# Ordering two products into one PSUM bank: a VectorE copy as a fence, or a drain in TensorE's own queue

## The chip, the cores and the metric

The kernel runs on one core of a Trainium2 chip. The metric is the device time of one execution in microseconds (us); the time of a kernel is the median of several executions. Beside the times stands a profile of one execution: every instruction of every engine with its start and length. The engines are TensorE (PE in the profile, PEld for its weight loads, which share its queue), VectorE (DVE), ScalarE (ACT), GpSimd (POOL), and SyncE (SP), which issues the DMAs. Each has its own queue, in which instructions start in order; engines wait for each other through semaphores.

## What is computed

A retention layer over 8 batches, 8 heads, 576 positions and head width 64, and then a feed-forward block over its 4608 rows:

```python
scores = scale * np.matmul(q, k.transpose(0, 1, 3, 2))
ret = scores * Dmat[None, :, :, :]        # Dmat: gamma ** (i - j) below the diagonal, else 0
attn = np.matmul(ret, v)                  # -> x, one row of 512 for each batch and position
h = x @ w_in                              # 512 -> 1024
e = np.exp(h - h_max); sm = e / (np.sum(e, axis=-1, keepdims=True) + 1e-09)
solu = h * sm
ln = (solu - mu) / np.sqrt(var + 1e-06) * g_ln
out = ln @ w_out                          # 1024 -> 512
```

Inputs and output are float32; the kernel multiplies in float16 and sums in float32.

## The kernel before

The 576 positions of a batch are cut into chunks of 128 and a last one of 64. A pair n holds one chunk of each of two batches, four groups of five, so 20 pairs; every fifth is the short one. A pair gives two row tiles of 128 rows (a short pair gives one), 36 tiles m in all.

Inside a chunk retention is worked out directly, and what came before it enters through a running state (64 by 64 for each head) that decays from chunk to chunk. So x of a pair is the sum of two products, in the same PSUM bank:

- the state products, step `xs` (line 374): the decayed state s16 of the chunk before, times the turned q. They need neither scores nor masks of this pair. The first chunk of a batch has no state, so its x has no such product.
- the value products, step `xv` (line 432): the masked scores `ret` times v. They are 32 matmuls of a 64 by 64 weight block for a full pair, 16 for a short one or for one batch of pair 0.

PE's array is worked in quarters here (64*64 in the profile). For a head the two products take their weights from different rows and both write the same bank. The kernel keeps them apart: the last state product has written before the first value product starts. Before the change the step `fx` (line 393) sees to that: a VectorE copy of a few columns of the bank, which waits for the state products because it reads what they write, and which the value products wait for because they write what it reads. What it copies, the tile `fence`, is read by nobody.

Around it, for each pair: load q, k, v (lines 187 and 180); cast and scale them to float16 (`cast`, lines 216 and 219, mostly on GpSimd); turn q and k (line 242 on PE and `back` at lines 134 and 136 out of PSUM, or a DMA at line 265); score products (line 311); two masks on VectorE, `m0` and `m1` (line 346, tile ret); new states (line 408 on PE, `t` at line 454 on VectorE, `decay` at line 458). Then for each tile: copy x out of PSUM and turn it into weights (`xT`, lines 134 and 136), w_in products (line 517), row maximum (line 540, tile nm), exp (line 565), h times e (line 595, tile u), moments (lines 602, 609, 617, 624, 632), transposes (line 643) and their copy (uT), w_out products (line 669), scaling (lines 685 and 689), store (line 700). `warm` (line 775) multiplies zeros.

The order is written out by hand: PLAN is one list of words, `name:pair.half/banks` with an engine behind @, and `follow` calls the step of each word in turn. Every engine's queue holds its instructions in the order of that list; semaphores are put in where an instruction reads or overwrites what another engine made. 20 words are `fx`: one for the second half of pair 0 and one for each later pair. Some stand right behind their `xs`, others several words later, and between `fx` and `xv` there is mostly other work for PE. On VectorE most stand behind the pair's masks; those of pairs 4 and 13 stand ahead of another pair's mask, and that of pair 0 ahead of its own.

Of the kernel before, what the change touches and what calls it, by code (L numbers as in the profile page):

```python
# [33 lines left out]
def kernel(  # L34
# [357 lines left out]
    @step  # L392
    def fx(n, j, eng, bs):

        bs = [T["x", n, x] for x in meets(n, j)]
        nc.vector.tensor_copy(
            out=buf("fence", 0, 1, [P, 2, 4], FP)[:, 0 : len(bs)], in_=banks(bs)[:, :, 0:512:128]
        )

    @step  # L400
    def kp(n, j, eng, bs):
        k16, v16 = t16("k", n), t16("v", n)

        def one(x, s, hp):
            r = slice(64 * x, 64 * x + 64)
            o = pb[:, bs[x if j is None else 0], 0:256].rearrange("p (a d) -> p a d", a=4)
            for e in range(2):
                nc.tensor.matmul(
                    out=o[64 * e : 64 * e + 64, hp], lhsT=k16[r, s, 2 * hp + e],
                    rhs=v16[r, s, 2 * hp + e], start=s == 0 and hp == 0, stop=True,  # L410
                    skip_group_check=True,
                )
# [360 lines left out]
    def warm(k, j, eng, bs):  # L773
# [9 lines left out]
        xv:0.0/4 tq:0.1/6 qT:0.1@v t:0.0@s s16:0.0@v warm:4/7 xs:0.1/5 fx:0.1 xT:0@s sc:0.1/0123  # L783
        m0:0.1 gl cw:0.1@s mm1:0.0/67 cw:1.1@s mm1:0.1 m1:0.1 warm:7/4 xv:0.1 cw:2.0@v wo:0 cw:3.0@s
        xT:1@v kp:0.1/4 cw:2.1@s mm1:0.2 s32:0.0@g cw:3.1@s mm1:0.3 max:0 mm1:1/01 t:0.1 max:1 q:1@g
        k:1@g warm:7/3 tk:1/2 exp:0 solu:0 nmu:0 w1:0.0 exp:1 solu:1 nmu:1 uc:1 wo:1 kT:1@s tq:1/3
        qT:1@s warm:4/6 sc:1/4523 m1:1 wo:2 m0:1 v:1@g warm:1/0 kp:1/67 t:1.0@s lp:1/0 s16:1.0@g
        s32:1.0@g xs:1/1 fx:1 xv:1/2 g32 uc:0 ws:2@v sq:1 wo:3 ws:7@v ws:6@g lv:2 ws:1@s lk:2 ws:3@s
        uT:1@v w1:0.1 t:1.1 s16:0.1@g s32:0.1@g s32:1.1@g lp:0/3 w2:0.1 xT:2@s mm1:2/45 ws:4@v
        ws:0@s lq:2 ws:5@s mm2:1/2 v:2@g max:2 exp:2 solu:2 nmu:2 lk:3 mean/0 k:2@s pow:0.1 uc:2  # L790
        uT:0@v osb:1@s kp:2/67 t:2.0 evm@s ce:1 ce:2 warm:3/4 lp:2/0 q:2@g s32:2.0@g tk:2/4 sq:0
        w2:0.0 s16:2.0@g lv:3 kT:2@s tq:2/5 qT:2@s warm:3/2 sc:2/2345 t:2.1 m0:2 xT:3@s xs:2/67
        uT:2@s s16:1.1@g m1:2 k:3@s fx:2 mm1:3/01 max:3 v:3@g kp:3/23 t:3.0 xv:2 xT:4@s xT:5@v ce:4
        exp:3 solu:3 nmu:3 s32:3.0@g tk:3/4 t:3.1 pow:0.0 mm2:0/5 osb:0@s lq:4 uc:3 kT:3@s mm1:4/67
        lq:3 q:3@g tq:3/5 max:4 qT:3@s lp:3/0 uT:3@s mm2:2/1 sc:3/2345 ce:0 mm2:3/0 ce:6 exp:4
        solu:4 sq:3 m1:3 m0:3 sq:2 mm1:5/67 lk:5 k:5@s lv:5 q:4@g tq:4/2 s16:3.0@g lk:4 qT:4@s lq:7
        xs:3/45 v:5@g w1:1 w2:1 lq:5 k:4@g tk:4/3 pow:1 osb:2@s max:5 exp:5 fx:3 lv:6 warm:1/2 xv:3
        st:0 kp:5/12 kT:4@v xT:7@s v:6@g t:5.0@s nmu:4 uc:4 lp:4/3 sq:4 lk:6 xT:6@v mm1:6/45 lk:7
        solu:5 s32:5.0@g osb:3@s nmu:5 uT:4@s uc:5 max:6 sq:5 lv:4 mm1:7/67 lp:5/0 t:5.1 lq:6 lq:10
        q:5@g w1:2 exp:6 tq:5/1 max:7 st:1 uT:5@s s16:2.1@g tk:5/3 k:6@g lv:7 exp:7 mm2:4/2 qT:5@s  # L800
        solu:6 lp:6/0 uT:6@s sc:4/45 ce:3 w2:2 pow:2 osb:4@s solu:7 kT:5@s s16:5.0@g m0:4 nmu:6
        mm2:5/1 osb:5@s ce:5 nmu:7 s16:3.1@g xs:4/67 fx:4 sc:5/4523 m0:5 m1:5 v:4@g xv:4 xT:8@s
        xs:5/0 fx:5 ce:7 st:4 sq:6 lp:7/1 w1:3 uT:7@s st:2 lq:9 mm1:8/67 max:8 kp:6/23 st:3 sq:7
        xv:5/1 xT:9@s lq:8 q:6@g t:6.0@s s32:6.0@v t:6.1 s16:6.1@v lv:9 lk:9 exp:8 st:5 wx xT:10@s
        solu:8 nmu:8 w1:4 mm2:7/4 s16:6.0@g w2:3 pow:3 s32:5.1@g tk:6/5 kT:6@v mm1:9/23 max:9 sq:8
        w2:4 v:7@g pow:4 mm1:10/01 k:9@g tq:6/5 max:10 exp:9 solu:9 lv:8 qT:6@s mm2:6/6 s16:5.1@g
        osb:7@s q:7@g exp:10 osb:6@v st:6 lp:8/7 lk:8 nmu:9 lq:11 sc:6/4523 uT:8@s m0:6 sq:9 k:7@g
        xs:6/6 mm2:8/7 m1:6 lk:10 fx:6 xv:6/2 lv:10 solu:10 nmu:10 q:9@v kp:7/45 t:7.0 q:8@g lp:9/3
        s32:7.0@g xT:11@s tk:7/0 kT:7@s mm1:11/12 s16:7.0@v uT:9@v v:8@g lk:11 osb:8@s xT:12@s
        max:11 sq:10 w1:5 exp:11 w2:5 pow:5 t:7.1 lp:10/0 uT:10@v solu:11 mm1:12/67 lk:12 tq:7/3  # L810
        qT:7@s mm2:9/4 sc:7/0123 max:12 m0:7 k:8@g tk:8/5 osb:9@s mm2:10/4 lv:11 exp:12 w1:6 m1:7
        kT:8@s lp:11/5 solu:12 st:8 q:10@g osb:10@s xs:7/01 fx:7 uT:11@v tq:9/2 qT:9@s nmu:11 st:7
        tq:8/3 xv:7 xT:13@s kp:8/67 s32:6.1@v s16:7.1@v v:10@g lp:12/2 mm1:13/45 t:8.0 qT:8@s
        xT:14@v s16:8.0@g nmu:12 s32:8.0@v t:8.1 s16:8.1@v max:13 sq:12 st:9 lv:12 sc:8/0167 m1:8
        sq:11 w2:6 v:9@g m0:8 uT:12@s exp:13 solu:13 pow:6 mm2:11/3 osb:11@v mm2:12/2 xs:8/01 fx:8
        mm1:14/67 xv:8 max:14 osb:12@s lp:13/4 uT:13@v dq:10 xT:15@s tk:9/5 exp:14 kT:9@s mm1:15/23
        xT:16@v k:10@g lq:12 nmu:13 sq:13 solu:14 nmu:14 sc:9/45 m0:9 mm1:16/01 xs:9/67 lq:13 dk:10
        v:11@g lq:15 max:15 lk:13 sq:14 fx:9 exp:15 st:11 max:16 solu:15 nmu:15 st:10 q:11@g lp:14/4
        st:12 xv:9 xT:17@s k:11@g mm2:13/5 exp:16 dk:11 q:12@g kp:10/67 t:10.0@s uT:14@s dq:11 sq:15
        lq:14 w1:7 w2:7 pow:7 lv:14 solu:16 osb:13@s mm1:17/23 lp:15/4 s32:10.0@g t:10.1 uT:15@s  # L820
        sc:10/0167 max:17 exp:17 lp:16/5 uT:16@s mm2:14/4 m0:10 m1:10 lv:13 s16:10.0@g k:12@s lk:14
        lv:15 xs:10/5 dk:12 fx:10 kp:11/01 t:11.0@s s16:10.1@g solu:17 nmu:16 xv:10/6 xT:18@s k:13@g
        q:13@g s32:11.0@g t:11.1 xT:19@v mm1:18/67 lp:17/5 uT:17@s nmu:17 osb:14@v s32:11.1@g dq:12
        s32:10.1@g max:18 sc:11/2301 exp:18 m1:11 s16:11.0@g xs:11/4 m0:11 w1:9 st:13 mm2:15/5 dq:13
        mm1:19/01 solu:18 lp:18/2 fx:11 xv:11/3 sq:17 k:14@g w2:9 v:12@v max:19 s16:11.1@g sq:16
        xT:21@s mm2:16/6 xT:20@v w1:8 w2:8 st:14 pow:9 exp:19 solu:19 nmu:19 uT:18@s pow:8 q:14@g
        osb:16@s osb:15@s mm1:20/34 max:20 sc:12/6701 m1:12 m0:12 exp:20 mm2:17/2 v:13@g nmu:18
        st:16 mm2:18/5 dk:13 solu:20 w1:10 osb:17@v sq:18 st:15 kp:12/01 t:12.0 s32:12.0@v mm1:21/67
        t:12.1 max:21 v:14@g lv:16 s16:12.0@g lk:15 sq:19 w2:10 pow:10 k:15@g lp:19/4 uT:19@s
        tk:14/3 kT:14@v tq:14/2 qT:14@v s16:12.1@v nmu:20 xs:12/01 lq:16 exp:21 q:16@g fx:12 lk:16  # L830
        solu:21 nmu:21 w1:11 mm2:19/4 xv:12 du:21 kp:13/23 k:16@g t:13.0 s32:13.0@v t:13.1 osb:18@s
        lp:20/5 xT:22@s mm1:22/67 sq:21 xT:23@s sc:13/2301 max:22 m1:13 m0:13 uT:20@s q:15@g
        osb:19@s lq:17 exp:22 sq:20 st:18 mm1:23/45 max:23 exp:23 mm2:21/0 w2:11 pow:11 mm2:20/1
        solu:22 nmu:22 s16:13.0@g sq:22 solu:23 dk:15 nmu:23 xs:13/23 fx:13 sc:14/67 lv:17 m0:14
        s16:13.1@g xs:14/45 fx:14 xv:13 xT:24@s xv:14 xT:25@v v:15@g kp:15/67 xT:26@v st:17 osb:21@s
        v:17@v w1:12 t:15.0@s s16:15.0@g s32:15.0@v mm1:25/23 v:16@g t:15.1 s32:15.1@g osb:20@s
        max:25 sq:23 w2:12 st:19 pow:12 du:23 mm1:24/45 exp:25 max:24 exp:24 mm2:23/0 osb:23@s
        s16:15.1@v du:22 mm2:22/1 dq:15 solu:25 sc:15/6723 solu:24 nmu:24 dq:16 m1:15 m0:15 q:17@g
        xs:15/0 fx:15 mm1:26/45 max:26 kp:16/23 du:24 xv:15/6 xT:27@v osb:22@s t:16.0@s s32:16.0@g
        exp:26 lp:25/1 t:16.1 uT:25@s solu:26 xT:28@s nmu:25 lk:18 sq:24 k:18@g nmu:26 dk:16  # L840
        mm1:27/67 max:27 mm1:28/23 max:28 exp:27 lp:26/1 solu:27 uT:26@s sc:16/4501 m0:16 s16:16.0@g
        xs:16/6 sq:25 m1:16 fx:16 w1:14 mm2:24/7 lq:19 sq:26 exp:28 solu:28 nmu:28 xv:16/0 lk:17
# [83 lines left out]
```

## Time and profile before

| | us |
|---|---|
| median of 3 runs | 230.87 |
| lowest and highest run | 229.31, 231.76 |
| the profiled execution, its own time | 231.2 |
| its span, first to last instruction | 229.5 |
| VectorE's copies of x into xT (line 136, 12 of them), busy | 8.5 |
| masks (line 346, 38 of them), busy | 42.7 |
| value products (line 432, 576 matmuls), busy | 12.6 |
| state products (line 374, 256 matmuls), busy | 9.0 |

"Busy" is the time in which at least one instruction of the group ran. Matmuls overlap in the array and their ends are modelled, so 576 value products of 216 ns each are busy for 12.6 us only. The chain of waits is followed back from the last instruction: at each step to what released it, or to the instruction before it in its queue; its shares say which engine ended last and for how long. In a view that names gaps, "[0.51 <-PE pb L374]" is the time that the engine stood idle before the instruction and what ended it. A "q" behind an engine's name marks its sequencer, which issues the instructions and itself runs some, drains among them.

### The profile page before, as it was taken

The numbers are of one execution on the slowest core, as the hardware profiler recorded it, in microseconds if no ns is written. First come the engines' busy times: TensorE is split into PE (matmuls) and PEld (weight loads), VectorE is DVE, ScalarE is ACT, GpSimd is POOL, SyncE is SP. The second block draws the span as 40 slices with busy tenths as digits, with TensorE's granted clock in tenths as the row PEclk, the third lists the DMA queues.
The fourth block names the chain that finished last, engine by engine and source line by source line (L and its number), as shares of the span: only waits on it lengthen the run. The fifth ranks groups of instructions, "written<-read, shape, count | busy, mean of one in ns | idle before, by whom it ended". The sixth has DMA issues, their size and how long they took to land.

```text
span 229.5 us, 7260 instructions
## 1 busy us (share of the span) xinstructions
PE 210.5 (92%) x2994; PEld 115.1 (50%) x2994; DVE 198.0 (86%) x346; ACT 152.9 (67%) x267; POOL 133.2 (58%) x181
## 2 busy tenths in 40 slices
PE   7999798999999999998998999998978689999992
PEld 2454543654565456564555544644434345555461
DVE  4568967999998899899999889999998988797971
ACT  2354647568898786657689566786547867857861
POOL 2585658887677498484687366487834083630230
PEclk9999979999999999999999999999999999999998
DMA  6999999999676999999898999999949997907044
GB/s 124 261 322 253 320 286 246 268 231 312 147 227 194 256 215 312 286 274 246 120 325 140 223 224 204 299 188 299 128 82 159 239 203 225 237 3 141 0 184 137
DMA packets 93265, 49.00 MB, mean 214 GB/s; under 512 B 37680, under 2 KB 87088, under 8 KB 93104
## 3 DMA queue, kind: packets, MB, share of 16 engines
q1 hardware_dynamic: 93088, 48.51, 94.0%
q8 instruction: 23, 0.38, 0.7%
q14 instruction: 10, 0.08, 0.1%
q10 hardware_dynamic: 144, 0.03, 0.1%
HBM read 32.54 MB, written 9.44 MB: 183 GB/s over the span
## 4 chain that ended last, share of the span: by engine, by line
PE 43%; DVE 31%; issue 7%; POOL 6%; DMA 6%; SPq 3%; ACT 3%; DVEq 0%; ACTq 0%; POOLq 0%
PE pb L517 15%; PE pb L669 12%; DVE ret L346 8%; DVE u L595 6%; DVE nm L540 5%; PE pb L775 5%; DMA ring<-in_k_dram 3%; PE pb L432 3%; DMA ring<-in_v_dram 3%; PE pb L643 2%; POOL v L219 2%; DVE w_mid L767 2%; PE pb L242 2%; PE pb L374 2%; POOL s L458 1%
## 5 line engine op out<-in xcount | busy, mean ns | idle before, releaser
L517 PE MATMUL pb<-w_in,xT 128*128 128x512 f16 x232 | 56.0, 388 | 3.0 <-ACT xT L134 1.3
L669 PE MATMUL pb<-w_mid,uT 128*128 128x512 f16 (+1 forms) x248 | 55.5, 373 | 0.0
L565 ACT ACTIVATE e<-pb,nm 128x1024 f32<-128x1024 f32 (+1 forms) x37 | 40.5, 1095 | 20.6 <-DVE nm L540 19.9
L540 DVE TENSOR_REDUCE nm<-pb 128x1 f32<-128x1024 f32 x35 | 42.6, 1219 | 7.0 <-PE pb L517 6.6
L595 DVE SCALAR_TENSOR_TENSOR u<-pb,e 128x1024 f16<-128x1024 f32 (+1 forms) x37 | 43.8, 1187 | 2.6 <-ACT e L565 2.3
L219 POOL TENSOR_TENSOR v<-ring,small 128x512 f16<-128x512 f32 (+1 forms) x34 | 37.3, 1114 | 10.7 <-DMA ring<-in_v_dram 6.2
L346 DVE TENSOR_TENSOR ret<-pb,keep 128x1024 f16<-128x1024 f32 (+2 forms) x38 | 42.7, 1158 | 0.8 <-PE pb L311 0.5
L517 PEld LDWEIGHTS <-xT 128*128 128x128 f16 x280 | 25.9, 99 | 34.1 <-ACT xT L134 2.6
L669 PEld LDWEIGHTS <-uT 128*128 128x128 f16 x296 | 27.6, 98 | 29.3 <-issue 0.6
L617 ACT ACTIVATE sq<-u,nmu 128x1024 f16<-128x1024 f16 (+1 forms) x31 | 34.9, 1125 | 4.3 <-DVE nmu L602 2.8
L219 POOL TENSOR_TENSOR q<-ring,small 128x512 f16<-128x512 f32 (+1 forms) x34 | 35.5, 1063 | 3.8 <-DMA ring<-in_q_dram 3.8
L458 POOL TENSOR_TENSOR s<-ts,small 128x256 f16<-128x256 f32 (+1 forms) x41 | 26.5, 659 | 15.5 <-DVE ts L454 8.1
L134 ACT CAST xT<-pb 128x512 f16<-128x512 f32 x24 | 17.1, 723 | 16.3 <-PE pb L432 16.2
L632 POOL TENSOR_TENSOR rs<-w,mhalf 128x2 f32<-128x2 f32 (+1 forms) x22 | 14.6, 664 | 19.2 <-DVE w L624 17.6
L689 ACT ACTIVATE osb<-pb,rs 128x512 f32<-128x512 f32 x26 | 17.7, 691 | 7.5 <-POOL rs L632 3.8
L136 POOL CAST k<-ring 128x1024 f16<-128x1024 f32 (+1 forms) x14 | 13.3, 948 | 14.6 <-DMA ring<-in_k_dram 13.8
L775 PE MATMUL pb<-zeros 128*128 128x512 f16 x58 | 17.2, 433 | 1.2 <-DVE zeros L874 1.2
L311 PE MATMUL pb<-qT,kT 64*64 64x128 f16 (+1 forms) x576 | 13.4, 217 | 3.5 <-DMA kT<-k 1.3
L591 POOL TENSOR_TENSOR w<-s 128x2 f32<-128x2 f32 (+1 forms) x22 | 4.8, 220 | 18.2 <-ACT e L565 18.2
L134 ACT COPY uT<-pb 128x512 f32<-128x512 f32 (+1 forms) x22 | 12.7, 577 | 3.7 <-PE pb L643 3.5
L311 PEld LDWEIGHTS <-kT 64*64 64x64 f16 x576 | 10.0, 106 | 9.7 <-issue 5.3
L643 PE MATMUL pb<-ident,u 128*128 128x128 f16 x184 | 13.8, 220 | 0.0
...
## 6 DMA issues: line engine op xcount, KB each, us to landing
...
```

What stands on the lines that cost most here:

```text
L134: nc.scalar.copy(out=out, in_=in_)
L219: vec(eng).tensor_tensor(out=t[:, s], in0=src[:, s], in1=by, op=ALU.mult)
L311: nc.tensor.matmul(out=scores(n, bs, e, hp, s)[c], lhsT=kt[r, s, hp, c], rhs=qt[r, 0:ns, hp, c], start=True, stop=True,)
L346: nc.vector.tensor_tensor(out=out, in0=src, in1=by, op=ALU.mult)
L458: vec(eng).tensor_tensor(out=s, in0=state("ts", n, x, FP), in1=gs.unsqueeze(2).to_broadcast([P, 4, D]), op=ALU.mult,)
L517: nc.tensor.matmul(out=pb[:, bs[i]], lhsT=s[:, d], rhs=w[:, d, i * 512 : (i + 1) * 512], start=r == 1, stop=r == 4,)
L540: nc.vector.tensor_reduce(out=tiny("nm", m, j), in_=h_of(m, j), axis=AX.X if j is not None else AX.XY, op=ALU.max, negate=True,)
L565: nc.scalar.activation(out=like_h(e_of(m), j), in_=h_of(m, j), func=ACT.Exp, bias=tiny("nm", m), accum_out=tiny("s", m, j),)
L595: nc.vector.scalar_tensor_tensor(out=like_h(u_of(m), j), in0=h_of(m, j), scalar=1.0, in1=like_h(e_of(m), j), op0=ALU.mult, op1=ALU.mult, a ...
L617: nc.scalar.activation(out=buf("sq", 0, 1, [P, DFF], F16)[:, cols(j)], in_=uc_of(m)[:, cols(j)], func=ACT.Square, accum_out=tiny("ss", m, ...
L669: nc.tensor.matmul(out=pb[:, bs[0], 0:w], lhsT=ut(m)[:, c], rhs=(w_out16 if m < RAW else w_mid16)[:, c, a : a + w], start=c == 0, stop=c = ...
L775: nc.tensor.matmul(out=pb[:, bs[0]], lhsT=zeros[:, 0:P], rhs=zeros, start=True, stop=True)
```

## The change

The step `fx` and its 20 words in PLAN go. In `xv` a drain of TensorE is put ahead of the matmuls wherever x already holds a state product; only the first half of pair 0 has none. PLAN is otherwise the same, word for word, so PE's matmuls and weight loads and the instructions of ScalarE, GpSimd and SyncE keep their order, and VectorE's queue loses 20 copies. The value products still wait for the masks and for v; a wait that was for the copy becomes one for the mask ahead of it. The second half of the value products of pair 2 then waits for the second mask by itself. Ten of the 20 drains stand behind matmuls on the whole array (128*128), ten behind matmuls on quarters (64*64).

```diff
     @step
-    def fx(n, j, eng, bs):
-
-        bs = [T["x", n, x] for x in meets(n, j)]
-        nc.vector.tensor_copy(
-            out=buf("fence", 0, 1, [P, 2, 4], FP)[:, 0 : len(bs)], in_=banks(bs)[:, :, 0:512:128]
-        )
-
-    @step
     def kp(n, j, eng, bs):
...
     @step
     def xv(n, j, eng, bs):
         new = [x for x in both(j) if ("x", n, x) not in T]
+        if len(new) < len(both(j)):
+
+            nc.tensor.drain()
         for x, b in zip(new, bs):
             T["x", n, x] = b
...
-        xs:1/1 fx:1 xv:1/2 g32 uc:0 ws:2@v sq:1
+        xs:1/1 xv:1/2 g32 uc:0 ws:2@v sq:1
```

More of the change, by code (lines that the diff above doesn't have):

```diff
@@ L782 @@
         warm:2/4 sc:0.0/2301 m0:0.0 v:0.1@g lv:1 warm:4/5 tk:0.1/4 kT:0.1@s kp:0.0/5 m1:0.0 warm:3/6
[L783 to L842, printed above, removed]
@@ L843 @@
-        xT:29@s q:19@v k:17@g xT:30@s kp:17/45 t:17.0 s32:17.0@v sq:28 lk:19 w1:13 w2:14 w2:13
-        pow:13 st:20 osb:24@s mm1:29/01 max:29 s32:16.1@g t:17.1 lv:18 mm1:30/23 max:30 exp:29
-        lp:28/6 solu:29 exp:30 st:21 dq:17 uT:28@s mm2:25/7 nmu:27 osb:25@s dk:17 sc:17/4501 k:19@s
-        m0:17 st:24 tk:18/6 pow:14 mm2:26/7 m1:17 s16:17.0@g xs:17/01 fx:17 sq:27 st:22 v:18@g
-        kp:18/45 kT:18@s xv:17 xT:31@s xT:32@s nmu:29 sq:29 w1:16 w1:15 s16:17.1@g du:27 solu:30
-        nmu:30 osb:26@v w2:15 s16:16.1@g pow:15 mm2:28/6 osb:28@s t:18.0 st:25 mm1:31/23 s32:18.0@v
@@ L849 @@
-        t:18.1 s16:18.1@g sq:30 max:31 exp:31 mm1:32/01 max:32 lq:18 w2:16 tk:19/7 kT:19@s tq:19/4
-        qT:19@s q:18@g s16:18.0@g tq:18/5 pow:16 solu:31 exp:32 du:29 solu:32 mm2:27/6 lp:30/7
-        qT:18@s uT:30@s sc:18/2345 m1:18 m0:18 xs:18/01 fx:18 st:23 osb:27@v mm2:29/7 lv:19 v:19@g
-        sc:19/23 m0:19 xv:18 xs:19/45 fx:19 st:26 st:27 lp:32/6 xv:19 w1:17 xT:33@s xT:34@v uT:32@s
-        nmu:31 sq:31 nmu:32 xT:35@v sq:32 mm1:33/23 max:33 mm1:34/01 max:34 exp:33 solu:33 exp:34
-        st:28 mm1:35.0/6 mm1:35.1/4 mm2:30/5 w1:18.1 w2:17 pow:17 nmu:33 max:35.0 max:35.1 nmm:35
@@ L855 @@
-        du:31 solu:34 nmu:34 mm2:31/2 osb:31@v mm2:32/3 lp:34/2 st:31 osb:29@s st:29 sq:33 exp:35.1
-        exp:35.0 solu:35.1 lp:35.1/7 solu:35.0 sadd:35 suadd:35 sq:34 osb:30@s w2:18.1 uT:34@s
-        w1:18.0 nmu:35 w2:18.0 lp:35.0/6 uT:35.0@v st:30 pow:18.0 osb:32@v lp:33/0 sq:35.1 mm2:34/1
-        pow:18.1 sq:35.0 uT:35.1@s mm2:35.0/4 uT:33@v mm2:33/5 st:32 ssadd:35 w1:19 w2:19 pow:19
-        osb:35.0@v osb:34@v st:35.0 st:34 mm2:35.1/4 osb:33@s osb:35.1@v st:33 st:35.1
+        xv:0.0/4 tq:0.1/6 qT:0.1@v t:0.0@s s16:0.0@v warm:4/7 xs:0.1/5 xT:0@s sc:0.1/0123 m0:0.1 gl
@@ new lines @@
+        cw:0.1@s mm1:0.0/67 cw:1.1@s mm1:0.1 m1:0.1 warm:7/4 xv:0.1 cw:2.0@v wo:0 cw:3.0@s xT:1@v
+        kp:0.1/4 cw:2.1@s mm1:0.2 s32:0.0@g cw:3.1@s mm1:0.3 max:0 mm1:1/01 t:0.1 max:1 q:1@g k:1@g
+        warm:7/3 tk:1/2 exp:0 solu:0 nmu:0 w1:0.0 exp:1 solu:1 nmu:1 uc:1 wo:1 kT:1@s tq:1/3 qT:1@s
+        warm:4/6 sc:1/4523 m1:1 wo:2 m0:1 v:1@g warm:1/0 kp:1/67 t:1.0@s lp:1/0 s16:1.0@g s32:1.0@g
+        xs:1/1 xv:1/2 g32 uc:0 ws:2@v sq:1 wo:3 ws:7@v ws:6@g lv:2 ws:1@s lk:2 ws:3@s uT:1@v w1:0.1
@@ new lines @@
+        t:1.1 s16:0.1@g s32:0.1@g s32:1.1@g lp:0/3 w2:0.1 xT:2@s mm1:2/45 ws:4@v ws:0@s lq:2 ws:5@s
+        mm2:1/2 v:2@g max:2 exp:2 solu:2 nmu:2 lk:3 mean/0 k:2@s pow:0.1 uc:2 uT:0@v osb:1@s kp:2/67
+        t:2.0 evm@s ce:1 ce:2 warm:3/4 lp:2/0 q:2@g s32:2.0@g tk:2/4 sq:0 w2:0.0 s16:2.0@g lv:3
+        kT:2@s tq:2/5 qT:2@s warm:3/2 sc:2/2345 t:2.1 m0:2 xT:3@s xs:2/67 uT:2@s s16:1.1@g m1:2
+        k:3@s mm1:3/01 max:3 v:3@g kp:3/23 t:3.0 xv:2 xT:4@s xT:5@v ce:4 exp:3 solu:3 nmu:3
+        s32:3.0@g tk:3/4 t:3.1 pow:0.0 mm2:0/5 osb:0@s lq:4 uc:3 kT:3@s mm1:4/67 lq:3 q:3@g tq:3/5
@@ new lines @@
+        max:4 qT:3@s lp:3/0 uT:3@s mm2:2/1 sc:3/2345 ce:0 mm2:3/0 ce:6 exp:4 solu:4 sq:3 m1:3 m0:3
+        sq:2 mm1:5/67 lk:5 k:5@s lv:5 q:4@g tq:4/2 s16:3.0@g lk:4 qT:4@s lq:7 xs:3/45 v:5@g w1:1
+        w2:1 lq:5 k:4@g tk:4/3 pow:1 osb:2@s max:5 exp:5 lv:6 warm:1/2 xv:3 st:0 kp:5/12 kT:4@v
+        xT:7@s v:6@g t:5.0@s nmu:4 uc:4 lp:4/3 sq:4 lk:6 xT:6@v mm1:6/45 lk:7 solu:5 s32:5.0@g
+        osb:3@s nmu:5 uT:4@s uc:5 max:6 sq:5 lv:4 mm1:7/67 lp:5/0 t:5.1 lq:6 lq:10 q:5@g w1:2 exp:6
+        tq:5/1 max:7 st:1 uT:5@s s16:2.1@g tk:5/3 k:6@g lv:7 exp:7 mm2:4/2 qT:5@s solu:6 lp:6/0
@@ new lines @@
+        uT:6@s sc:4/45 ce:3 w2:2 pow:2 osb:4@s solu:7 kT:5@s s16:5.0@g m0:4 nmu:6 mm2:5/1 osb:5@s
+        ce:5 nmu:7 s16:3.1@g xs:4/67 sc:5/4523 m0:5 m1:5 v:4@g xv:4 xT:8@s xs:5/0 ce:7 st:4 sq:6
+        lp:7/1 w1:3 uT:7@s st:2 lq:9 mm1:8/67 max:8 kp:6/23 st:3 sq:7 xv:5/1 xT:9@s lq:8 q:6@g
+        t:6.0@s s32:6.0@v t:6.1 s16:6.1@v lv:9 lk:9 exp:8 st:5 wx xT:10@s solu:8 nmu:8 w1:4 mm2:7/4
+        s16:6.0@g w2:3 pow:3 s32:5.1@g tk:6/5 kT:6@v mm1:9/23 max:9 sq:8 w2:4 v:7@g pow:4 mm1:10/01
+        k:9@g tq:6/5 max:10 exp:9 solu:9 lv:8 qT:6@s mm2:6/6 s16:5.1@g osb:7@s q:7@g exp:10 osb:6@v
@@ new lines @@
+        st:6 lp:8/7 lk:8 nmu:9 lq:11 sc:6/4523 uT:8@s m0:6 sq:9 k:7@g xs:6/6 mm2:8/7 m1:6 lk:10
+        xv:6/2 lv:10 solu:10 nmu:10 q:9@v kp:7/45 t:7.0 q:8@g lp:9/3 s32:7.0@g xT:11@s tk:7/0 kT:7@s
+        mm1:11/12 s16:7.0@v uT:9@v v:8@g lk:11 osb:8@s xT:12@s max:11 sq:10 w1:5 exp:11 w2:5 pow:5
+        t:7.1 lp:10/0 uT:10@v solu:11 mm1:12/67 lk:12 tq:7/3 qT:7@s mm2:9/4 sc:7/0123 max:12 m0:7
+        k:8@g tk:8/5 osb:9@s mm2:10/4 lv:11 exp:12 w1:6 m1:7 kT:8@s lp:11/5 solu:12 st:8 q:10@g
+        osb:10@s xs:7/01 uT:11@v tq:9/2 qT:9@s nmu:11 st:7 tq:8/3 xv:7 xT:13@s kp:8/67 s32:6.1@v
@@ new lines @@
+        s16:7.1@v v:10@g lp:12/2 mm1:13/45 t:8.0 qT:8@s xT:14@v s16:8.0@g nmu:12 s32:8.0@v t:8.1
+        s16:8.1@v max:13 sq:12 st:9 lv:12 sc:8/0167 m1:8 sq:11 w2:6 v:9@g m0:8 uT:12@s exp:13
+        solu:13 pow:6 mm2:11/3 osb:11@v mm2:12/2 xs:8/01 mm1:14/67 xv:8 max:14 osb:12@s lp:13/4
+        uT:13@v dq:10 xT:15@s tk:9/5 exp:14 kT:9@s mm1:15/23 xT:16@v k:10@g lq:12 nmu:13 sq:13
+        solu:14 nmu:14 sc:9/45 m0:9 mm1:16/01 xs:9/67 lq:13 dk:10 v:11@g lq:15 max:15 lk:13 sq:14
+        exp:15 st:11 max:16 solu:15 nmu:15 st:10 q:11@g lp:14/4 st:12 xv:9 xT:17@s k:11@g mm2:13/5
@@ new lines @@
+        exp:16 dk:11 q:12@g kp:10/67 t:10.0@s uT:14@s dq:11 sq:15 lq:14 w1:7 w2:7 pow:7 lv:14
+        solu:16 osb:13@s mm1:17/23 lp:15/4 s32:10.0@g t:10.1 uT:15@s sc:10/0167 max:17 exp:17
+        lp:16/5 uT:16@s mm2:14/4 m0:10 m1:10 lv:13 s16:10.0@g k:12@s lk:14 lv:15 xs:10/5 dk:12
+        kp:11/01 t:11.0@s s16:10.1@g solu:17 nmu:16 xv:10/6 xT:18@s k:13@g q:13@g s32:11.0@g t:11.1
+        xT:19@v mm1:18/67 lp:17/5 uT:17@s nmu:17 osb:14@v s32:11.1@g dq:12 s32:10.1@g max:18
+        sc:11/2301 exp:18 m1:11 s16:11.0@g xs:11/4 m0:11 w1:9 st:13 mm2:15/5 dq:13 mm1:19/01 solu:18
@@ new lines @@
+        lp:18/2 xv:11/3 sq:17 k:14@g w2:9 v:12@v max:19 s16:11.1@g sq:16 xT:21@s mm2:16/6 xT:20@v
+        w1:8 w2:8 st:14 pow:9 exp:19 solu:19 nmu:19 uT:18@s pow:8 q:14@g osb:16@s osb:15@s mm1:20/34
+        max:20 sc:12/6701 m1:12 m0:12 exp:20 mm2:17/2 v:13@g nmu:18 st:16 mm2:18/5 dk:13 solu:20
+        w1:10 osb:17@v sq:18 st:15 kp:12/01 t:12.0 s32:12.0@v mm1:21/67 t:12.1 max:21 v:14@g lv:16
+        s16:12.0@g lk:15 sq:19 w2:10 pow:10 k:15@g lp:19/4 uT:19@s tk:14/3 kT:14@v tq:14/2 qT:14@v
+        s16:12.1@v nmu:20 xs:12/01 lq:16 exp:21 q:16@g lk:16 solu:21 nmu:21 w1:11 mm2:19/4 xv:12
@@ new lines @@
+        du:21 kp:13/23 k:16@g t:13.0 s32:13.0@v t:13.1 osb:18@s lp:20/5 xT:22@s mm1:22/67 sq:21
+        xT:23@s sc:13/2301 max:22 m1:13 m0:13 uT:20@s q:15@g osb:19@s lq:17 exp:22 sq:20 st:18
+        mm1:23/45 max:23 exp:23 mm2:21/0 w2:11 pow:11 mm2:20/1 solu:22 nmu:22 s16:13.0@g sq:22
+        solu:23 dk:15 nmu:23 xs:13/23 sc:14/67 lv:17 m0:14 s16:13.1@g xs:14/45 xv:13 xT:24@s xv:14
+        xT:25@v v:15@g kp:15/67 xT:26@v st:17 osb:21@s v:17@v w1:12 t:15.0@s s16:15.0@g s32:15.0@v
+        mm1:25/23 v:16@g t:15.1 s32:15.1@g osb:20@s max:25 sq:23 w2:12 st:19 pow:12 du:23 mm1:24/45
@@ new lines @@
+        exp:25 max:24 exp:24 mm2:23/0 osb:23@s s16:15.1@v du:22 mm2:22/1 dq:15 solu:25 sc:15/6723
+        solu:24 nmu:24 dq:16 m1:15 m0:15 q:17@g xs:15/0 mm1:26/45 max:26 kp:16/23 du:24 xv:15/6
+        xT:27@v osb:22@s t:16.0@s s32:16.0@g exp:26 lp:25/1 t:16.1 uT:25@s solu:26 xT:28@s nmu:25
+        lk:18 sq:24 k:18@g nmu:26 dk:16 mm1:27/67 max:27 mm1:28/23 max:28 exp:27 lp:26/1 solu:27
+        uT:26@s sc:16/4501 m0:16 s16:16.0@g xs:16/6 sq:25 m1:16 w1:14 mm2:24/7 lq:19 sq:26 exp:28
+        solu:28 nmu:28 xv:16/0 lk:17 xT:29@s q:19@v k:17@g xT:30@s kp:17/45 t:17.0 s32:17.0@v sq:28
@@ new lines @@
+        lk:19 w1:13 w2:14 w2:13 pow:13 st:20 osb:24@s mm1:29/01 max:29 s32:16.1@g t:17.1 lv:18
+        mm1:30/23 max:30 exp:29 lp:28/6 solu:29 exp:30 st:21 dq:17 uT:28@s mm2:25/7 nmu:27 osb:25@s
+        dk:17 sc:17/4501 k:19@s m0:17 st:24 tk:18/6 pow:14 mm2:26/7 m1:17 s16:17.0@g xs:17/01 sq:27
+        st:22 v:18@g kp:18/45 kT:18@s xv:17 xT:31@s xT:32@s nmu:29 sq:29 w1:16 w1:15 s16:17.1@g
+        du:27 solu:30 nmu:30 osb:26@v w2:15 s16:16.1@g pow:15 mm2:28/6 osb:28@s t:18.0 st:25
+        mm1:31/23 s32:18.0@v t:18.1 s16:18.1@g sq:30 max:31 exp:31 mm1:32/01 max:32 lq:18 w2:16
@@ new lines @@
+        tk:19/7 kT:19@s tq:19/4 qT:19@s q:18@g s16:18.0@g tq:18/5 pow:16 solu:31 exp:32 du:29
+        solu:32 mm2:27/6 lp:30/7 qT:18@s uT:30@s sc:18/2345 m1:18 m0:18 xs:18/01 st:23 osb:27@v
+        mm2:29/7 lv:19 v:19@g sc:19/23 m0:19 xv:18 xs:19/45 st:26 st:27 lp:32/6 xv:19 w1:17 xT:33@s
+        xT:34@v uT:32@s nmu:31 sq:31 nmu:32 xT:35@v sq:32 mm1:33/23 max:33 mm1:34/01 max:34 exp:33
+        solu:33 exp:34 st:28 mm1:35.0/6 mm1:35.1/4 mm2:30/5 w1:18.1 w2:17 pow:17 nmu:33 max:35.0
+        max:35.1 nmm:35 du:31 solu:34 nmu:34 mm2:31/2 osb:31@v mm2:32/3 lp:34/2 st:31 osb:29@s st:29
@@ L860 @@
+        sq:33 exp:35.1 exp:35.0 solu:35.1 lp:35.1/7 solu:35.0 sadd:35 suadd:35 sq:34 osb:30@s
+        w2:18.1 uT:34@s w1:18.0 nmu:35 w2:18.0 lp:35.0/6 uT:35.0@v st:30 pow:18.0 osb:32@v lp:33/0
+        sq:35.1 mm2:34/1 pow:18.1 sq:35.0 uT:35.1@s mm2:35.0/4 uT:33@v mm2:33/5 st:32 ssadd:35 w1:19
+        w2:19 pow:19 osb:35.0@v osb:34@v st:35.0 st:34 mm2:35.1/4 osb:33@s osb:35.1@v st:33 st:35.1
     """
```

## The prediction, made before the changed kernel was run

> **What bounds the kernel now.** I read the page's busy times first, then its chain of waits by engine and line, then the two stretches in which VectorE (DVE) is fullest.
>
> ```profile
> span 229.5 us, 7260 instructions
> PE 210.5 (92%) x2994; PEld 115.1 (50%) x2994; DVE 198.0 (86%) x346; ACT 152.9 (67%) x267; POOL 133.2 (58%) x181
> PE 43%; DVE 31%; issue 7%; POOL 6%; DMA 6%; SPq 3%; ACT 3%; DVEq 0%; ACTq 0%; POOLq 0%
> ```
> ```profile
> 40.00:58.00 18.00, 16.88 (x242) 9.56 (x239) 17.90 (x27) 11.43 (x19) 13.75 (x16) 1.00 1.15 264
> 150.00:175.00 25.00, 21.91 (x348) 11.43 (x346) 24.15 (x38) 15.76 (x30) 15.99 (x20) 1.00 1.00 172
> ```
>
> The bound changes hands. TensorE (PE) carries 43% of the chain and VectorE 31%; in the two stretches of the second fence (start, length, PE busy, PEld, DVE busy, ...) VectorE is busy for 17.90 of 18.00 us and 24.15 of 25.00 us while PE has 1.1 and 3.1 us to spare. So the copy has to be priced where VectorE ends last, and the drain where PE does. The profiled execution took 231.2 us by its own clock, 1.7 us more than its span; the median of the runs is 230.87.
>
> **What the change removes.** Twenty small copies leave VectorE. First the view of the tile they write, then the waits of PE, then the chain in stretches.
>
> ```profile
> L396 DVE COPY fence<-pb x20: 145/155/167, 14.7 to 207.7; 128x8 f32<-128x8 f32 x12, 128x4 f32<-128x4 f32 x8
>   PE pb L374: 2.1, 4
> ```
> ```profile
> PE pb L432 <- DVE ret L346: 0.8, 2, 0.6
> ```
> ```profile
> 28.27 0.14 DVE fence L396
> 132.94 0.07 DVE fence L396
> 194.14 0.04 DVE fence L396
> ```
> ```profile
> 14.72 0.16 DVE L396 COPY fence<-pb 128x4 f32<-128x4 f32 x1 [0.51 <-PE pb L374]
> 70.43 0.17 DVE L396 COPY fence<-pb 128x8 f32<-128x8 f32 x1 [0.33 <-PE pb L374]
> ```
>
> A copy takes 155 ns, 20 of them 3.1 us; but neighbours overlap, and where it lies on the chain behind busy VectorE it costs 0.07 us (the row at 132.94; the one at 28.27, the first, is the dearest). The chain holds six such pieces, from the first at 28.27 to the last at 194.14, together 0.48 us: that is the gain I count. VectorE also stood idle 2.1 us, four times, until the state products (L374) were done and the copy could go, and work queued behind it stood too. At 14.72 and 70.43, and at 124.65 and 194.14 (rows further down), the chain around it runs on PE or GpSimd, so the idle VectorE held nothing up and I count nothing for it; were VectorE the bound there, it would be worth up to 2.1 us. And PE's list of waits for the value products (L432) names the masks (ret), not the copy: the masks stay, and there is little wait to remove on PE.
>
> **What it adds.** A drain in PE's own queue, directly ahead of the value products, in 20 places (all pairs but the first half of pair 0). Nothing can pass it: every weight load and matmul behind it, and through them the copies xT (L134, L136), the w_in matmuls and the row maximum, wait until all earlier matmuls have written. The trace has one such drain with a full queue, at the program's end.
>
> ```profile
> L921 PEldq DRAIN  x2: 13/1004/1995, 223.4 to 229.1; - x2
> L921 PEldq EVENT_SEMAPHORE  x2: 51/51/51, 228.9 to 229.4; - x2
> ```
> ```profile
> 222.82 2.55 PE L669 MATMUL pb<-w_mid,uT 128*128 128x512 f16 x15
> 225.41 0.48 DVE L685 TENSOR_SCALAR osb<-pb,rs 128x256 f32<-128x256 f32 x1 [1.40 <-PE pb L669]
> ```
>
> PE's sequencer reached it at 223.4 and left it 1995 ns later, at 225.4; the last matmul ends at 222.82 + 2.55 = 225.37 and its reader on VectorE starts at 225.41. So a drain ends about 0.05 us after the last matmul. The restart behind it the trace does not show. Near it are the sequencer's step from one instruction to the next (from 228.9 + 0.05 to the second drain at 229.1, so about 0.1 us) and, below, nothing at all. I take 0.15 us from the end of the last matmul to the first value product, with 0.05 and 0.25 as ends.
>
> What this loses depends on what stands ahead of the drain, and so on how early the values start today.
>
> ```profile
> 133.00 0.62 PE L643 MATMUL pb<-ident,u 128*128 128x128 f16 x8
> 133.55 0.47 PE L432 MATMUL pb<-ret,v 64*64 64x128 f16 x18
> ```
> ```profile
> 73.83 0.45 PE L408 MATMUL pb<-v,k 64*64 64x64 f16 x32
> 74.10 0.62 PE L432 MATMUL pb<-ret,v 64*64 64x128 f16 x32
> ```
>
> Behind work on the whole array (128*128) the values start at 133.55, 0.07 us before that work's modelled end at 133.62; with a drain they start 0.15 us after it, a loss of 0.22 us. Behind work in the same quarters (64*64) they start at 74.10 while the last matmul ends at 74.28: a loss of 0.18 + 0.15 = 0.33 us. Where a mask, a load's cast or the copy itself opens the values, it is less. These are the value products on the chain:
>
> ```profile
> 17.60 0.56 PE pb L432 x16
> 59.27 0.63 PE pb L432 x32
> 70.98 0.32 PE pb L432 x16
> 74.28 0.45 PE pb L432 x32
> 110.31 0.63 PE pb L432 x32
> 116.61 0.25 PE pb L432 x16
> 124.86 0.68 PE pb L432 x30
> 147.84 0.57 PE pb L432 x32
> 158.81 0.52 PE pb L432 x31
> 194.37 0.62 PE pb L432 x32
> 206.86 0.45 PE pb L432 x32
> 208.12 0.25 PE pb L432 x16
> ```
> ```profile
> 69.48 1.46 POOL v L219
> ```
> ```profile
> 124.32 0.46 PE L408 MATMUL pb<-v,k 64*64 64x64 f16 x28
> 124.65 0.16 DVE L396 COPY fence<-pb 128x4 f32<-128x4 f32 x1 [0.22 <-PE pb L374]
> 193.91 0.42 PE L408 MATMUL pb<-v,k 64*64 64x64 f16 x32
> 194.14 0.17 DVE L396 COPY fence<-pb 128x8 f32<-128x8 f32 x1 [1.04 <-PE pb L374]
> 194.36 0.36 PE L432 MATMUL pb<-ret,v 64*64 64x128 f16 x11
> ```
>
> By the plan, six of the twelve stand behind 128*128 work (17.60, 59.27, 110.31, 116.61, 147.84, 208.12): 6 x 0.22 = 1.32 us. Three stand behind 64*64 work with nothing else late (74.28, 158.81, 206.86): 3 x 0.33 = 0.99 us. At 70.98 GpSimd's cast of v ends at 70.94 and opens them: 0. At 124.86 the copy ended at 124.81 and opened the bulk of them; with a drain it is 124.78 + 0.15 = 124.93, a loss of 0.07. At 194.36 it is 194.33 + 0.15 = 194.48, a loss of 0.12. Together 2.50 us. The other eight drains lie beside the chain: the one in the first of the two stretches above stands behind 64*64 work, and its 0.33 us is covered by the 1.1 us that PE has spare; without that cover it would be paid too.
>
> **The sum.** 2.50 - 0.48 = +2.0 us: 231.2 becomes 233.2, and the median 230.87 becomes 232.9. With 0.05 us instead of 0.15 the twelve cost 0.72 + 0.69 + 0.02 = 1.43, so +0.95; with 0.25 they cost 1.92 + 1.29 + 0.39 = 3.60, so +3.1. The forecast's own range is 231.8 to 234.0.
>
> The Trainium skill's page "TensorE: Matmul & The Clock Gate", in Single matmul latency and Back-to-back issue gap, speaks against the change: a lone matmul of 128 columns takes (398 + 128)/2.4 = 219 ns where one in a stream takes 55.6, since a stream hides the array's emptying. By that, twelve drains cost an estimated 12 x 0.164 = 2.0 us before any restart, where my rows give 2.5 with it.
>
> The skill's page "TensorEngine Tiling (Array Packing)", Key Properties, says that a change of tiling mode empties TensorE by itself. The rows at 133.55 agree only in part: the first value product starts 0.07 us before the modelled end of the last transpose. Were the rule whole, the six places behind 128*128 work would lose 0.15 and not 0.22 us, and the sum would be +1.6.
>
> **Rivals.** *VectorE was the bound, and the drains hide.* Then the 20 slots of 0.07 us come back, 1.4 us, and with them up to all 2.1 us of idle time: 1.4 to 3.5 us faster, 227.4 to 229.5, in the middle 228.4. For it: the two full stretches above, and a queue that no longer stops for PE. Against: in those stretches the chain meets the copy for under 0.1 us at a time, and twelve drained places carry the chain on PE.
>
> *The drain also takes away PE's lead.* The drain at 223.4 stood 2 us ahead of the matmuls, so today the values' loads and matmuls wait in the queue before they are due; behind a drain they come as the sequencer makes them. The two rows from 73.83 to 74.10 + 0.62 = 74.72 are 64 pairs in 0.89 us. If half of them lay ready, the sequencer needs up to 0.89/32 = 0.028 us a pair, and the 32 pairs of the values take 0.89 us instead of 0.62: 0.27 us more in each full place. With eight full and four half places on the chain that is 10 x 0.27 = 2.7 us more, +4.7 in all: 235.6. It decides from a sequencer slower than 0.62/32 = 0.019 us a pair. Against: those 64 pairs run without a pause between them.
>
> *The drain does nothing while the engine runs on.* Then only 0.48 us is gained: 230.4. The 1995 ns of the drain at the end speak against it.
>
> **How the numbers follow.** I give the forecast 0.46, the lost lead 0.24, VectorE as the bound 0.27, the idle drain 0.03. A measurement of this kernel can tell about 1% (2.3 us) from no change. The forecast's +2.0 lies just inside that: 0.19 slower, 0.27 same. The lost lead is slower. VectorE's case reaches past 228.6 with 0.20 and stays inside with 0.07; the idle drain is the same. So faster 0.20, same 0.37, slower 0.43. The range goes from 228.4, the middle of VectorE's case, to 235.6, the lost lead's time; that leaves out about 0.13 below and 0.07 above.
>
> **What would show it.** Twenty drains on PE's sequencer, each ending about 0.05 us after the last matmul ahead of it, and the next value product about 0.1 us after that; PE's idle time ahead of L432 up from 1.1 us. A lost lead would show as pairs spread wider than today's 0.62 us for 32 at 74.10; VectorE as the bound as u and ret (L595, L346) starting earlier by more than 0.1 us a pair of tiles and PE's places unmoved at the end. It would be wrong if the restart cost far more than 0.25 us, or if the chain left PE for VectorE at the twelve places.

## The result, and the profile after

| | before | after |
|---|---|---|
| median of 12 runs, us | 229.69 | 231.13 |
| lowest and highest, us | 228.52, 231.78 | 229.94, 232.37 |
| profiled execution, own time and span, us | 231.2, 229.5 | 231.3, 229.5 |

The changed kernel takes 1.0081 times as long, with a 95% interval from 1.0055 to 1.0107: 1.3 to 2.5 us slower. The two profiled executions show none of it, since their spans are equal: the execution taken for the kernel before was one of its longer ones. So the profiles are read here place by place, and the total is left to the runs.

The page of the changed kernel, with its busy times and the chain by engine; lines of the code have moved up, so line 427 is the value products, 512 the w_in products, 417 the drain:

```profile
span 229.5 us, 7252 instructions
PE 211.2 (92%) x2994; PEld 114.9 (50%) x2994; DVE 194.4 (85%) x326; ACT 152.7 (67%) x267; POOL 132.9 (58%) x181
PE 38%; DVE 25%; POOL 11%; DMA 10%; issue 8%; ACT 4%; SPq 3%; DVEq 0%; ACTq 0%; POOLq 0%
```

VectorE is busy for 3.6 us less (198.0 to 194.4), and the span has not moved. Its list of waits says where part of the time went. Before (engine and line, what it waited for, total us, times, longest):

```profile
DVE nm L540 <- PE pb L517: 6.6, 12, 1.0
DVE fence L396 <- PE pb L374: 2.1, 4, 1.0
DVE ret L346 <- PE pb L311: 0.5, 1, 0.5
```

After:

```profile
DVE nm L535 <- PE pb L512: 8.5, 13, 1.7
DVE ret L346 <- PE pb L311: 1.8, 3, 0.7
```

The copies' 2.1 us of waiting are gone, but the masks now wait 1.3 us longer for the score products and the row maxima 1.9 us longer for the w_in products. In this execution VectorE's time came back as waiting for PE.

On PE, the groups of the value products, before and after (busy, mean of one in ns, idle time of the engine just before them and what ended it):

```profile
L432 PE MATMUL pb<-ret,v 64*64 64x128 f16 (+1 forms) x576 | 12.6, 216 | 1.1 <-DVE ret L346 0.8
```
```profile
L427 PE MATMUL pb<-ret,v 64*64 64x128 f16 (+1 forms) x576 | 12.2, 216 | 2.8 <-DVE ret L346 0.8 <-issue 0.4 <-POOL v L219 0.2
```

The wait for the masks is the same 0.8 us; PE's idle time ahead of the values rose by 1.7 us. And these are the two places at which the prediction worked out its prices, in the timeline after (line 638 is the transposes, 400 the state update):

```profile
133.27 0.62 PE L638 MATMUL pb<-ident,u 128*128 128x128 f16 x8
133.97 0.53 PE L427 MATMUL pb<-ret,v 64*64 64x128 f16 x24
73.95 0.45 PE L400 MATMUL pb<-v,k 64*64 64x64 f16 x32
74.53 0.64 PE L427 MATMUL pb<-ret,v 64*64 64x128 f16 x32
```

Behind the transposes the values now start 133.97 - 133.89 = 0.08 us after their modelled end, where they started 0.07 us before it: 0.15 us lost. Behind the state update they start 74.53 - 74.40 = 0.13 us after it, where they started 0.18 us before it: 0.31 us lost.

The drains themselves, as the sequencer's instructions (shortest, median and longest in ns):

```profile
L417 PEldq DRAIN  x20: 307/610/2792, 15.1 to 207.1; - x20
```

Each begins when the sequencer reaches it, while matmuls ahead of it are still queued (for up to 2.8 us), and its length is mostly that lead. In the trace's records, to the nanosecond, a drain ends 21 to 48 ns after the modelled end of the last matmul where that was on the whole array, and 46 to 145 ns after it on quarters. The Trainium skill's page "PSUM — Partial Sum Buffer", Engine vs sequencer instructions, says that a drain waits for the engine to go fully idle; the 20 records agree. After the drain the first weight load starts 52 or 53 ns later and the first value product 59 or 60 ns later, unless a mask or a load holds it.

The wait for the masks itself is also unchanged in PE's list (before 0.8, 2, 0.6):

```profile
PE pb L427 <- DVE ret L346: 0.8, 2, 0.6
```

The chain of waits after the change runs through eleven places of the value products that have a drain. Eight of them are among the prediction's twelve; these three were beside the chain before:

```profile
45.82 0.69 PE pb L427 x32
133.97 0.64 PE pb L427 x32
182.52 0.69 PE pb L427 x32
```

Those at 17.60, 70.98, 74.28 and 206.86 of the kernel before are no longer on it. Which places the chain meets is thus a matter of the single execution, and of tenths of a microsecond between engines.

### The profile page after: what moved, and what is told of

Read it like the earlier page. It is cut to its first block, busy times and chain, and to the rows that moved or that the text cites. A ratio compares the mean times of both kernels' runs of the same rounds, so it can differ in the third digit from the quotient of the medians.

```text
span 229.5 us, 7252 instructions
## 1 busy us (share of the span) xinstructions
PE 211.2 (92%) x2994; PEld 114.9 (50%) x2994; DVE 194.4 (85%) x326; ACT 152.7 (67%) x267; POOL 132.9 (58%) x181
## 4 chain that ended last, share of the span: by engine, by line
PE 38%; DVE 25%; POOL 11%; DMA 10%; issue 8%; ACT 4%; SPq 3%; DVEq 0%; ACTq 0%; POOLq 0%
PE pb L512 15%; PE pb L664 12%; DVE ret L346 6%; DVE u L590 6%; DMA ring<-in_moe_w_in_dram 5%; DMA ring<-in_v_dram 4%; DVE nm L535 4%; POOL q L219 4%; PE pb L427 3%; POOL v L219 3%; SPq L187 2%; PE pb L638 2%; POOL s L453 2%; DVE w_mid L762 2%; PE pb L374 2%
## 5 line engine op out<-in xcount | busy, mean ns | idle before, releaser
L427 PE MATMUL pb<-ret,v 64*64 64x128 f16 (+1 forms) x576 | 12.2, 216 | 2.8 <-DVE ret L346 0.8
```

The costliest lines, as they stand in the source:

```text
L427: nc.tensor.matmul(out=o[out_half(n, x, e), hp, 0:w], lhsT=v16[r, s, 2 * hp + e], rhs=kept(n, x, e, hp, s), start=x in new and s == 0 and ...
```

## The experiments

**The copies and the drains together.** The kernel before, with the drain added in `xv`:

```diff
         new = [x for x in both(j) if ("x", n, x) not in T]
+        if len(new) < len(both(j)):
+            nc.tensor.drain()
```

> The 20 copies stay and the 20 drains are added: the drains' cost by itself. My theory (drains cost 1.9 to 2.5 us on the chain, the copies' slots give back 0.5): 1.0085 to 1.011 times the kernel before, and 0.0015 to 0.003 above the changed kernel's 1.0081. Rival 1 (VectorE was the nearer bound, the copies' 20 slots and their 2.1 us of waiting were worth 1.4 to 3.5 us, and the drains cost that much more): 1.014 to 1.024. Rival 2 (the drains hide and the loss has another cause): 1.000 to 1.003.

Measured: 1.0109 times the kernel before, interval 1.0072 to 1.0146 (6 runs against 22). That is my theory's value; the lower end of the first rival, 1.014, still lies just inside the interval, and the second rival is excluded. The drains cost about 2.5 us by themselves. What the copies' removal gives back, 1.0109 - 1.0081, is some 0.6 us; with both intervals it can be anything from nothing to 1.7 us.

**VectorE's slots.** In the changed kernel, with the words `fx` left in PLAN, four small instructions of VectorE at each place of the old copy, which wait for no other engine:

```diff
+    @step
+    def fx(n, j, eng, bs):
+        for i in range(4):
+            nc.vector.tensor_copy(
+                out=buf("fence", i, 4, [P, 2, 4], FP).rearrange("p a c -> p (a c)"),
+                in_=keep[:, 4, 0:8],
+            )
```

> The changed kernel with four small VectorE copies of a constant in SBUF at each of the 20 places where the copy stood; they wait for no other engine and nobody waits for them. 80 slots of some 0.07 us are 5.6 us on VectorE. My theory (a slot counts only where VectorE carries the chain, six places): 4 x 0.45 = 1.8 us more than the changed kernel, 1.015 to 1.018 times the kernel before. Rival 1 (VectorE is the bound throughout): 5 us more, 1.03. Rival 2 (VectorE has room everywhere): 1.007 to 1.010.

Measured: 1.0254, interval 1.0202 to 1.0305, nearer to the first rival. But the price of a slot was not the one I had put in. The view of the tile they write:

```profile
L395 DVE COPY fence<-keep x80: 153/160/1019, 13.4 to 210.1; 128x8 f32<-128x8 f32 x80
```

The longest of these copies of 8 elements took 1019 ns, where the old copies out of PSUM never took more than 167. From the first of each four to what follows them the 20 places add up to 11.5 us. So this run doubles the load, and its expected values don't apply to it. (Against that load, the 4.0 us by which it is slower than the changed kernel are again a part only.) The run was made again with an instruction that does not stall:

```diff
-            nc.vector.tensor_copy(
-                out=buf("fence", i, 4, [P, 2, 4], FP).rearrange("p a c -> p (a c)"),
-                in_=keep[:, 4, 0:8],
-            )
+            nc.vector.tensor_reduce(
+                out=buf("fence", i, 4, [P, 1], FP), in_=keep[:, 4, 0:8], axis=AX.X, op=ALU.max
+            )
```

> As the run with free copies, but each of the 80 VectorE instructions is a reduction of 8 elements from SBUF, because the copies of that run took up to 1.0 us each where GpSimd was at work, together 11.5 us and not 5.6. If the reductions keep to some 0.07 us a slot, 5.8 us on VectorE. My theory (a slot counts only where VectorE carries the chain, six places): 1.015 to 1.018 times the kernel before. Rival 1 (VectorE is the bound throughout): 1.03. Rival 2 (VectorE has room everywhere): 1.007 to 1.010.

```profile
L395 DVE TENSOR_REDUCE fence<-keep x80: 144/151/158, 14.2 to 209.0; 128x1 f32<-128x8 f32 x80
```

All 80 keep to 144 to 158 ns, and four take 0.27 us from start to next start, 0.068 us a slot: 5.4 us of VectorE's time in all. Measured: 1.0128, interval 1.0084 to 1.0173. Over the changed kernel that is 0.0047 or 1.1 us, a fifth of what was put on VectorE; with both intervals it is at most 2.3 us, and nothing isn't excluded. The value is a little under my 1.015; 1.03 is excluded, and the second rival's 1.010, by which VectorE has room everywhere, lies in the interval too. So VectorE isn't the bound throughout, and 20 single slots are worth about a quarter of 1.1 us, if anything.

**The step of a drain.** Five drains in a row in place of one:

```diff
-            nc.tensor.drain()
+            for _ in range(5):
+                nc.tensor.drain()
```

> The changed kernel with five drains in a row in each of the 20 places. Nothing is left to empty for the later four, so each adds only the sequencer's step and restart, 0.05 us by the 52 ns that lie between a drain's end and the next weight load: 0.2 us a place. My theory (the twelve places on the chain pay): 12 x 0.2 = 2.4 us more than the changed kernel, 1.018 times the kernel before. Rival 1 (all 20 places pay, on the chain or off it): 4 us more, 1.026. Rival 2 (steps cost nothing, only the emptying does): 1.008.

```profile
L418 PEldq DRAIN  x100: 8/8/2333, 15.2 to 212.3; - x100
```

Here the median drain takes 8 ns, since behind the first there is nothing to empty. But in the records one starts some 70 ns after the other, and from the end of the first to the next weight load there are 337 ns instead of 52: 0.285 us more in each place, not the 0.2 that I had assumed. On PE this shows as idle time in which it waits for nothing that the profile knows ("issue"), 5.2 us where the changed kernel had 0.4:

```profile
L428 PE MATMUL pb<-ret,v 64*64 64x128 f16 (+1 forms) x576 | 12.2, 216 | 8.1 <-issue 5.2 <-DVE ret L346 1.7 <-ACT sq L613 0.4
```

Measured: 1.0263, interval 1.0212 to 1.0313, 0.0182 or 4.2 us over the changed kernel. By the expected values this is the first rival's 1.026, but those were worked out with a step that was too cheap. With 0.285 us the twelve places of the chain make 3.4 us (1.0230, inside the interval), and all 20 make 5.7 us (1.033, outside it). The changed kernel's own spread widens the range to 2.9 to 5.5 us, ten to 19 places; the chain of this run's own profile meets 14. So the cost of the steps is real and twelve is possible, but the number isn't shown, nor that a drain beside the chain is free.

**Fewer of either.** First the drains of the second half of pair 0 and of pairs 5 and 14 left out, whose value products are ordered behind the state products by other waits (those of pair 14 by pair 13's drain, which stands behind both pairs' state products):

```diff
-        if len(new) < len(both(j)):
+        if n in (1, 2, 3, 4, 6, 7, 8, 9, 10, 11, 12, 13, 15, 16, 17, 18, 19) and len(new) < len(both(j)):
 
             nc.tensor.drain()
```

> The changed kernel without the drains of the second half of pair 0 and of pairs 5 and 14, whose order other waits already give; 17 drains. My theory: at 17.8 us and at 74.4 us a drain on the chain goes, 0.15 and 0.30 us: 1.006 times the kernel before, 0.002 below the changed kernel. Rival (the cost is not paid place by place, but comes from PE's sequencer stopping at all): all of 20 places count alike, 3/20 of the loss goes: 1.007.

Measured: 1.0072, interval 1.0039 to 1.0105. Both expectations lie in it; three drains are too few to be seen. Then, without any drain, two copies left out of the kernel before (the words `fx:0.1` and `fx:5` of PLAN):

> The kernel before without the copies of the second half of pair 0 and of pair 5, whose order other waits already give; no drain. My theory: neither copy lies on the chain, so 0.998 to 1.001 times the kernel before, and the hybrid's 0.9946 comes from its six drains in place of copies. Rival (the gain of the hybrid is that of any eight copies fewer on VectorE): two copies are a quarter of it, 0.9987.

Measured: 1.0008, interval 0.9981 to 1.0036. Two copies off the chain are worth nothing that can be seen, which fits the theory; the rival's 0.9987 lies in the interval too.

**A hybrid.** The kernel before with drains where VectorE or a mask sets the pace, copies in the other places that need either:

```diff
         new = [x for x in both(j) if ("x", n, x) not in T]
+        if n in (1, 2, 6, 7, 11, 15):
+            nc.tensor.drain()
...
-        xs:1/1 fx:1 xv:1/2 g32 uc:0
+        xs:1/1 xv:1/2 g32 uc:0
```

(The words for the second half of pair 0 and for pairs 2, 5, 6, 7, 11 and 15 go likewise.)

> Drains in the six places where VectorE or a mask sets the pace (pairs 1, 2, 6, 7, 11, 15), copies in twelve places where PE carries the chain, and neither in the second half of pair 0 and in pair 5, whose value products already wait for something that came after the state products. My theory: the six copies' 0.48 us on the chain go and no drain lies on it: 0.997 to 0.999 times the kernel before. Rival 1 (VectorE was the bound everywhere): 0.995 or less for these eight copies. Rival 2 (every drain costs, on the chain or off it): 1.002 to 1.005.

Measured: 0.9946, interval 0.9913 to 0.9978, a median of 228.84 us (12 runs) against 229.99: faster than both kernels, and by 1.2 us where 0.48 were expected. As a number this is the first rival's (0.995 or less), not my theory's. The profile shows another reason. From the first value product of pair 13 to the first of pair 15 the hybrid takes 12.15 us, and the profiles of all other kernels take 13.39 or more (before 13.42, after 13.39). The timeline of VectorE and GpSimd in that stretch, of the kernel before and of the hybrid:

```profile
160.57 1.74 DVE L219 TENSOR_TENSOR v<-ring,small 128x512 f16<-128x512 f32 x2
161.15 0.61 POOL L458 TENSOR_TENSOR s<-ts,small 128x256 f16<-128x256 f32 x1 [1.22 <-ACT ts L134]
161.72 2.67 POOL L219 TENSOR_TENSOR v<-ring,small 128x512 f16<-128x512 f32 x2
162.23 1.26 DVE L458 TENSOR_TENSOR s<-ts,small 128x256 f32<-128x256 f32 x1
```
```profile
160.39 1.28 DVE L219 TENSOR_TENSOR v<-ring,small 128x512 f16<-128x512 f32 x2
161.25 0.90 POOL L460 TENSOR_TENSOR s<-ts,small 128x256 f16<-128x256 f32 x1 [1.51 <-ACT ts L134]
161.59 0.83 DVE L460 TENSOR_TENSOR s<-ts,small 128x256 f32<-128x256 f32 x1
162.11 2.22 POOL L219 TENSOR_TENSOR v<-ring,small 128x512 f16<-128x512 f32 x2
```

The row of VectorE's two scalings of v begins with the first; the second starts 0.60 us later in the records of both. Before, GpSimd's state decay (161.15) starts 0.58 us after the first, just ahead of the second; the two take 1.74 us, and the decay on VectorE behind them 1.26. In the hybrid GpSimd's decay starts 0.86 us after the first, when the second runs already; the two take 1.28 us, and now it is GpSimd's instruction that is the longer one, 0.90 us. VectorE is ahead by more than 0.8 us at the end of its decay. In the profiles of seven of the eight other kernels GpSimd's decay starts 0.24 to 0.58 us after the first scaling and the second takes 1.10 to 1.14 us; in the hybrid's it takes 0.69. (In the eighth, the run with free copies, GpSimd's decay starts with the first scaling and itself takes 2.08 us.) To see whether this belongs to the hybrid or to one execution, it was profiled again:

> The hybrid once more for a second profile. In the first one the stretch from the value products of pair 14 to those of pair 15 took 12.1 us, where the other profiles have 13.4 us, because VectorE's scaling of v and its state decays met no GpSimd instruction. If that belongs to the hybrid's order of events (theory 1), the stretch is again within 0.3 us of 12.1; if it was chance in one execution (theory 2), it is 13.2 to 13.6 and the hybrid's gain comes from the drains and copies alone.

```profile
159.47 1.28 DVE L219 TENSOR_TENSOR v<-ring,small 128x512 f16<-128x512 f32 x2
160.19 1.03 POOL L460 TENSOR_TENSOR s<-ts,small 128x256 f16<-128x256 f32 x1 [1.37 <-ACT ts L134]
160.66 0.84 DVE L460 TENSOR_TENSOR s<-ts,small 128x256 f32<-128x256 f32 x1
```

The same order again (0.72 us after the first), and the stretch takes 12.14 us. That execution took 228.0 us. GpSimd's decay waits for ScalarE, which copies the new state (ts) out of PSUM behind a scaling (osb). In both of the hybrid's profiles that scaling waited for a store to land, 0.36 and 0.23 us; in the kernel before it followed the copy of x ahead of it within 0.1 us (the first two rows are the hybrid's, the third is the kernel before's):

```profile
160.22 0.69 ACT L691 ACTIVATE osb<-pb,rs 128x512 f32<-128x512 f32 x1 [0.36 <-DMA out_dram<-osb]
159.16 0.69 ACT L691 ACTIVATE osb<-pb,rs 128x512 f32<-128x512 f32 x1 [0.23 <-DMA out_dram<-osb]
160.12 0.69 ACT L689 ACTIVATE osb<-pb,rs 128x512 f32<-128x512 f32 x1
```

So by the profiles a late store put GpSimd behind VectorE's second scaling, and the hybrid's 1.2 us are about what this stretch gives, 1.25 us; no run changed that order by itself. Up to the first value product of pair 13 the hybrid's two profiles (158.46 and 157.53 us) show no such lead over that of the run with 18 copies (157.64). Whether the hybrid's choice between drains and copies gives anything beside the stretch isn't shown, nor which of its edits makes the store late.

## Why the prediction was right, point by point

**The total.** 232.9 us was forecast from 230.87, that is +2.0 us or 0.9%; 0.81% was measured, 1.9 us. The forecast's own range, counted from the 229.69 of the twelve runs, is 230.6 to 232.8, and 231.13 lies in it. The loss lies inside the bound of 1%, where the forecast had put the larger part of its own chance; over all its cases the prediction had given a little more to a loss beyond 1% (0.43) than to one inside (0.37).

**The mechanism.** That the drains cost time on PE is shown: added alone they cost 2.5 us, and more of them in the same places cost more.

**The price of a drain** was the unknown, taken as 0.15 us from the end of the last matmul to the first value product, with 0.05 and 0.25 as ends. It is 0.08 us in seven places behind whole-array work and 0.11 in three, and 0.11 to 0.20 us behind quarters where no mask or load holds the values. Two steps make it up. The restart was too dear: 0.1 us by the sequencer's step near the end of the program, 0.06 measured. The end of the drain, 0.05 us behind the last matmul by the one drain of the kernel before, is 0.02 to 0.05 us behind whole-array work, but up to 0.15 behind quarters. With the measured prices the twelve places give 0.96 us (six behind 128*128), 0.90 (three behind 64*64) and 0.25 (the two opened by a copy), 2.1 us in place of 2.5, and with the 0.48 us of the copies +1.6 us: inside the measured interval of 1.3 to 2.5. That the lost overlap (0.07 and 0.18 us) is about as large a part of it as the drain and its restart shows at 133.97 and 74.53 above.

The prediction's estimate of 0.164 us from the Trainium skill's page "TensorE: Matmul & The Clock Gate" (Single matmul latency, Back-to-back issue gap) is near the 0.18 us of overlap lost behind quarters and too much behind whole-array work, where 0.07 us was lost. The spacing that goes into it, 55.6 ns, agrees: the eight transposes at 133.00 of the kernel before follow each other mostly 56 ns apart.

**The count of places** is the part that the total doesn't test. The place at 45.82 is on the changed kernel's chain, although the prediction had taken its 0.33 us as covered by the 1.1 us that PE had to spare. Worked out the same way from the two profiles, the eleven places on the changed kernel's own chain lose 1.9 us and all 20 places lose 2.8; less 0.48 that is +1.4 and +2.4, and both lie in the measured interval too. That the sum came so near with the twelve of one execution is in part luck.

**The gain of the copies**, 0.48 us by six pieces of the chain, fits two runs and is shown by neither: 1.0109 against 1.0081 gives some 0.6 us with an interval that includes zero, and four slots for one cost 1.1 us, 0.27 us for each set of 20, with an interval that includes zero as well. That VectorE's 2.1 us of idle time were worth little fits its waits: 3.2 us came back as waits of the masks and row maxima for PE.

**The rivals.** VectorE as the bound throughout would have made the kernel faster, and 5.4 us of slots cost 5 us; it is slower, and they cost 1.1. The lost lead was to show as pairs spread wider: behind a drain the 32 pairs take 0.64 us in each of the 15 full places, and 0.62 to 0.64 before where nothing interrupts them; the sequencer keeps up. The idle drain falls with the records, in which every drain ends after the last matmul ahead of it.

**What stays open.** The count of places that pay, and so whether a drain beside the chain costs anything. Twelve is what the chain of one execution said; the run with five drains in a row allows ten to 19 places at 0.285 us.
